# One first transfer cut into four, and a small one moved to the other queue

## The chip, the cores and the metric

The kernel runs on 1 core of one Trainium2 chip. The metric is the device time of one execution, in microseconds (us). Before the change it is 245.59 us, the median of 3 runs (245.19 to 245.89).

## The reference, cut to what matters

One block of a decoder works on one new token for each of 4 sequences: D is 512, there are 32 query heads, 8 heads of keys and values, a window of the last 2048 cached positions, and a hidden width of 1792. Everything is float32.

```python
mod = (_silu(c) @ w_mod).reshape(c.shape[0], 6, 1, -1)
sa, ca, ga, sb, cb, gb = (mod[:, i] for i in range(6))
h = _layernorm(x) * (1 + ca) + sa
x = x + ga * attention(h, k_cache, v_cache, wq, wo)
h = _layernorm(x) * (1 + cb) + sb
x = x + gb * ((_silu(h @ w1) * (h @ w3)) @ w2)
```

With four tokens there is little arithmetic for each byte of the weights and of the cache. What the change touches is the way in which the first weights, w_mod's part for sa and ca, reach the core together with x and c.

## The kernel before, in words

All large operands pass through one ring of buffers, the pool `stream`, with SLOTS = 5 tiles of 128 partitions by 8192 floats (4 MB each), all with the tag "w". `plan` (line 47) lists them in the order of their use: wma (sa and ca of w_mod, 128 x 4096), the two halves of wq, then for each of the 8 groups of heads its keys and its values, with the two halves of wo in between, then wmb, w1, w3, wmc and w2. `load_ahead(name)` (line 56) issues transfers on SP's queue until five tiles from the named one on have been asked for; a tile whose slot is still in use waits, on SP, until the last reader of that slot is done. So the first call, for wma, issues wma, wq0, wq1, k0 and v0, and each further call issues one more. `cuts` splits a tile's transfer by columns into several: w3 comes in two halves and w2 in four pieces (`W3_CUTS`, `W2_CUTS`, lines 23 and 24). All other tiles come in one transfer with whole rows; a row of wma has 4096 floats, 16 KB, and one of wq, k or v 32 KB. The host has laid all arrays out so that a tile is one block of 128 rows.

x and c lie side by side in one array of 128 x 144 floats, `xc_in`. It is loaded into `xc_sb` by ACT's queue (line 77), beside SP's first transfer.

The work at the front goes in this order. DVE and GpSimd make the constants (`ident`, `same`, `avg`, `pick`, zeros). When xc_sb has landed, ACT takes exp(-c) (line 111) and DVE makes from it sc, which is silu(c) (lines 112 to 114), and the row sums of x (line 163). `norm` gives mean and variance of x with two products (lines 120 and 126). `mod_columns` (line 154) multiplies sc with wma in 16 products, over 4 blocks k of the 512 inputs and 4 blocks j of columns: the columns of wma are ordered by k first, so that a quarter of its columns is one k. `modulate` and `transposed` make hT (line 151), and only then does `project_q` (line 172) use wq. Then come the 8 groups: scores (line 204), softmax, values (line 232). After them come the output projection (line 193), the second norm, the two products of the hidden layer (line 283), wmc's product, and the last product with w2 (line 311), whose result is added and stored.

Every execution of line 64 is one transfer on SP's queue, and they are served in the order of their issue.

Of the kernel before, what the change touches and what calls it, by code (L numbers as in the profile page):

```python
# [8 lines left out]
F32 = mybir.dt.float32  # L9
# [5 lines left out]
P = 128  # L15
# [3 lines left out]
ROW = 8192  # L19
# [9 lines left out]
def block_kernel(ctx: ExitStack, tc: tile.TileContext, xc_in, w_mod_a, w_mod_b, w_mod_c, wq, k_t, v, wo, w1, w3, w2, out):  # L29
# [4 lines left out]
    nc = tc.nc  # L34
# [3 lines left out]
    stream = ctx.enter_context(tc.tile_pool(name="stream", bufs=SLOTS))  # L38
# [14 lines left out]
    plan += [("wmb", w_mod_b, None), ("w1", w1, None), ("w3", w3, W3_CUTS), ("wmc", w_mod_c, None), ("w2", w2, W2_CUTS)]  # L53
    tiles = {}

    def load_ahead(name):

        upto = [n for n, _, _ in plan].index(name) + SLOTS
        for n, src, cuts in plan[len(tiles) : upto]:
            t = stream.tile([P, ROW], F32, tag="w", name="w")  # L60
            size = src.shape[1]
            for a, b in zip(cuts[:-1], cuts[1:]) if cuts else ((0, 1),):
                step = size // cuts[-1] if cuts else size
                nc.sync.dma_start(t[:, a * step : b * step], src[:, a * step : b * step])
            tiles[n] = t[:, :size]
        return tiles[name]
# [7 lines left out]

    nc.scalar.preload_act_table_set("natural_log_exp_and_others")
    xc_sb = consts.tile([P, P + 16], F32, name="xc_sb")
    nc.scalar.dma_start(xc_sb, xc_in)
    x_sb, ct_sb = xc_sb[:, :P], xc_sb[:, P:]

    wma = load_ahead("wma")  # L80


# [103 lines left out]
    for half in range(2):  # L186
        wq_t = load_ahead(f"wq{half}")
        for i in range(4):
            project_q(4 * half + i, wq_t[:, i * 2048 : (i + 1) * 2048])
# [5 lines left out]
    def group(g):  # L195
        nonlocal wo_t
        q = qT[:, g]
        kv = load_ahead(f"k{g}").rearrange("p (t b n) -> p t b n", t=NT, b=B)
        mx = small.tile([P, NT], F32, name="mx")
        s_t = []  # L200
# [160 lines left out]
```

## Time and profile before

| what | us |
|---|---|
| median of 3 runs | 245.59 (245.19 to 245.89) |
| the profiled execution | 245.65 |
| its span, first to last instruction | 243.9 |
| TensorE (PE) busy | 170.2 |
| VectorE (DVE) busy | 51.3 |
| ScalarE (ACT) busy | 34.6 |
| first issue of w_mod_a on SP, first issue of xc on ACT | 0.73, 0.76 |
| first work on xc_sb | 9.16 |
| first product with wq | 18.79 |
| issue of the store of the result | 241.49 |

The span is what the views of the trace show; the time of the execution has 1.75 us more, outside of the instructions. In the views, a row of groups of work names the line, the engine and the operands ("L204 PE MATMUL s<-w,qT"). A "DMA" step in the chain of waits goes from the issue of a transfer to the moment at which it lets its reader go, and so holds the time that it stood in the queue. In the windows view a row gives, for a stretch of time, how long each engine was busy, with the number of its instructions, then the granted clock of TensorE, the busy share of the 16 DMA engines and the rate. A packet is counted, with its bytes and its whole duration, in the stretch in which it starts, so that a short stretch can show a share above 1.

### The profile page before, as it was taken

The numbers are of one execution on the slowest core, as the hardware profiler recorded it, in microseconds if no ns is written. First come the engines' busy times: TensorE is split into PE (matmuls) and PEld (weight loads), VectorE is DVE, ScalarE is ACT, GpSimd is POOL, SyncE is SP. The second block draws the span as 40 slices with busy tenths as digits, with TensorE's granted clock in tenths as the row PEclk, the third lists the DMA queues.
The fourth block names the chain that finished last, engine by engine and source line by source line (L and its number), as shares of the span: only waits on it lengthen the run. The fifth ranks groups of instructions, "written<-read, shape, count | busy, mean of one in ns | idle before, by whom it ended". The sixth has DMA issues, their size and how long they took to land.

```text
span 243.9 us, 2815 instructions
## 1 busy us (share of the span) xinstructions
PE 170.2 (70%) x1194; PEld 71.2 (29%) x1194; DVE 51.3 (21%) x163; ACT 34.6 (14%) x90; POOL 2.2 (1%) x9
## 2 busy tenths in 40 slices
PE   0178788789696969783867549677655654865984
PEld 0123353351334323341253002421321210232242
DVE  1330000003334151511231003312311400123210
ACT  2000100100404022040040000400400400000000
POOL 3000000000000000000000000000000000000000
PEclk9995555555998999998579575797995996795899
DMA  7999999999999999999999999999999999999991
GB/s 238 462 430 430 430 430 427 430 430 430 430 423 430 430 427 430 430 431 427 441 430 427 435 435 441 430 427 435 430 430 435 441 422 411 435 416 433 415 413 69
DMA packets 4619, 101.49 MB, mean 416 GB/s; under 512 B 512, under 2 KB 768, under 8 KB 1024
## 3 DMA queue, kind: packets, MB, share of 16 engines
q1 hardware_dynamic: 4464, 101.26, 97.1%
q8 instruction: 9, 0.15, 0.2%
q10 hardware_dynamic: 144, 0.07, 0.1%
q14 instruction: 2, 0.02, 0.0%
HBM read 101.26 MB, written 0.07 MB: 416 GB/s over the span
## 4 chain that ended last, share of the span: by engine, by line
DMA 53%; PE 39%; ACT 4%; DVE 2%; issue 1%; SPq 0%; ACTq 0%
DMA w<-k_t 18%; DMA w<-v 17%; DMA w<-w 10%; PE s L204 10%; PE o_ps L232 9%; DMA w<-wq 7%; PE bank L175 6%; PE bank L180 6%; PE bank L228 5%; ACT q_sb L177 2%; PE bank L244 2%; ACT p_sb L218 1%; DVE mx L205 1%; ACT o_sb L240 1%; PE y_ps L311 1%
## 5 line engine op out<-in xcount | busy, mean ns | idle before, releaser
L204 PE MATMUL s<-w,qT 128*32 128x512 f32 x256 | 40.1, 783 | 14.4 <-DMA w<-k_t 14.4
L232 PE MATMUL o_ps<-w,pT 128*16 128x512 f32 x256 | 32.2, 648 | 6.7 <-DMA w<-v 6.7
L228 PE MATMUL bank<-ident,p_sb 128*128 128x128 f32 x128 | 23.7, 329 | 15.4 <-ACT p_sb L218 15.2
L218 ACT ACTIVATE p_sb<-s,nm 128x512 f32<-128x512 f32 x32 | 21.6, 687 | 82.3 <-DVE nm L208 82.3
L205 DVE TENSOR_REDUCE mx<-s 128x1 f32<-128x512 f32 x32 | 22.1, 692 | 45.8 <-PE s L204 45.8
L228 PEld LDWEIGHTS bank<-ident,p_sb 128*128 128x128 f32 x128 | 17.2, 165 | 26.9 <-ACT p_sb L218 26.8
L204 PEld LDWEIGHTS s<-w,qT 128*32 128x32 f32 x256 | 9.2, 139 | 39.2 <-issue 23.5
L180 PEld LDWEIGHTS bank<-same,q_sb 128*128 128x128 f32 x64 | 14.3, 328 | 19.9 <-ACT q_sb L177 19.9
L180 PE MATMUL bank<-same,q_sb 128*128 128x4 f32 x64 | 15.0, 357 | 6.1 <-ACT q_sb L177 6.1
L175 PE MATMUL bank<-w,hT 128*32 128x512 f32 x64 | 15.5, 1058 | 0.7 <-DMA w<-wq 0.7
L232 PEld LDWEIGHTS o_ps<-w,pT 128*16 128x16 f32 x256 | 6.9, 102 | 27.4 <-issue 19.3
L241 DVE TENSOR_SCALAR o_sb<-o_ps,rl 128x256 f32<-128x256 f32 x8 | 3.9, 483 | 44.1 <-ACT o_sb L240 44.1
L244 PE MATMUL bank<-pick,o_sb 128*128 128x16 f32 x64 | 9.1, 268 | 5.1 <-ACT o_sb L240 5.1
L193 PE MATMUL a_ps<-w,oT 128*4 128x512 f32 x64 | 9.8, 758 | 3.6 <-DMA w<-wo 3.3
L229 DVE COPY pT<-bank 128x64 f32<-128x64 f32 x32 | 7.2, 224 | 24.3 <-PE bank L228 24.3
L244 PEld LDWEIGHTS bank<-pick,o_sb 128*128 128x128 f32 x64 | 8.3, 190 | 12.5 <-ACT o_sb L240 12.5
L240 ACT ACTIVATE o_sb<-o_ps,rl 128x256 f32<-128x256 f32 x8 | 3.8, 474 | 50.3 <-PE o_ps L232 50.3
L283 PE MATMUL pg<-w,h2T 128*4 128x512 f32 (+3 forms) x64 | 9.8, 654 | 0.4 <-DVE h2T L151 0.4
L177 ACT ACTIVATE q_sb<-bank 128x512 f32<-128x512 f32 x8 | 4.8, 597 | 34.3 <-PE bank L175 34.3
L120 PE MATMUL bank<-tot,avg 128*128 128x1 f32 x4 | 0.9, 304 | 12.2 <-DVE avg L89 10.6
L181 DVE COPY qT<-bank 128x64 f32<-128x64 f32 x8 | 1.8, 225 | 34.9 <-PE bank L180 34.9
L159 PE MATMUL bank<-w,sc 128*4 128x256 f32 (+5 forms) x96 | 8.4, 441 | 0.5 <-DVE sc L114 0.5
(75 smaller groups left out, 54.0 us busy)
## 6 DMA issues: line engine op xcount, KB each, us to landing
w<-k_t SPq DMA_DIRECT2D x8, 4096.0 KB, 39.7
w<-v SPq DMA_DIRECT2D x8, 4096.0 KB, 40.1
w<-wq SPq DMA_DIRECT2D x2, 4096.0 KB, 22.1
w<-wo SPq DMA_DIRECT2D x2, 4096.0 KB, 40.9
w<-w SPq DMA_DIRECT2D x1, 3584.0 KB, 41.2
w<-w SPq DMA_DIRECT2D x2, 1792.0 KB, 35.7
w<-w_mod_b SPq DMA_DIRECT2D x1, 3072.0 KB, 40.9
w<-w_mod_a SPq DMA_DIRECT2D x1, 2048.0 KB, 8.2
```

Of the source, the lines that this page charges most:

```text
L159: nc.tensor.matmul(pb[32 * j : 32 * j + rows(k), : n * P], sc[:, k, : rows(k)], wv[:, k, j, :], start=(k == 0), stop=(k == 3))
L175: nc.tensor.matmul(qp[32 * k : 32 * k + 32, :], hT[:, k, :], wt[:, k * 512 : (k + 1) * 512], start=True, stop=True)
L177: nc.scalar.mul(q_sb, qp, DH**-0.5)
L180: nc.tensor.matmul(qtp[:, i, :], q_sb[:, i * P : (i + 1) * P], same[:, :B], start=True, stop=True)
L193: nc.tensor.matmul(a_ps[32 * i : 32 * i + B, :], oT[:, g, i, :], wo_t[:, g % 4, i, :], start=(g == 0), stop=(g == G - 1))
L204: nc.tensor.matmul(s[32 * b : 32 * b + 32, :], q[:, b, :], kv[:, t, b, :], start=True, stop=True)
L205: nc.vector.reduce_max(mx[:, t : t + 1], s, axis=AX.X)
L218: nc.scalar.activation(p_sb[:, t, :], s_t[t], AF.Exp, bias=nm, accum_out=ls[:, t : t + 1])
L228: nc.tensor.transpose(pt[:, c * P : (c + 1) * P], p_sb[:, t, c * P : (c + 1) * P], ident)
L232: nc.tensor.matmul(o_ps[32 * b : 32 * b + NC * R, :], pT[:, t, b].rearrange("p c r -> p (c r)"), vt[:, t, b, :], start=(t == 0), stop=(t = ...
L244: nc.tensor.matmul(otp, o_sb[:, c * P : (c + 1) * P], pick[:, c].rearrange("p r b -> p (r b)"), start=(c == 0), stop=(c == NC - 1))
L283: nc.tensor.matmul(pg[32 * j : 32 * j + rows(k), :n], h2T[:, k, : rows(k)], ws[:, k, j * 512 : j * 512 + n], start=(k == 0), stop=(k == 3))
```

## The change

A new function `load_first` takes the first tile out of the ring, fills it by four transfers on SP's queue, each with a quarter of the columns of w_mod_a (128 rows of 1024 floats, 4 KB), and then issues the transfer of x and c on the same queue. ACT issues none. The tile is entered under the name wma, so that `load_ahead("wma")` that follows issues wq0, wq1, k0 and v0, as it did after wma before. Nothing else is changed.

```diff
+    def load_first():
+        t = stream.tile([P, ROW], F32, tag="w", name="w")
+        size = w_mod_a.shape[1]
+        for i in range(4):
+            nc.sync.dma_start(t[:, i * size // 4 : (i + 1) * size // 4], w_mod_a[:, i * size // 4 : (i + 1) * size // 4])
+        nc.sync.dma_start(xc_sb, xc_in)
+        tiles["wma"] = t[:, :size]
+
     def load_ahead(name):
...
     xc_sb = consts.tile([P, P + 16], F32, name="xc_sb")
-    nc.scalar.dma_start(xc_sb, xc_in)
     x_sb, ct_sb = xc_sb[:, :P], xc_sb[:, P:]
 
+    load_first()
     wma = load_ahead("wma")
```

## The prediction, made before the result was known

> **What bounds the kernel now.** I read the page first: the span, the busy times, the line of the DMA engines, and what the queues carried.
>
> ```profile
> span 243.9 us, 2815 instructions
> PE 170.2 (70%) x1194; PEld 71.2 (29%) x1194; DVE 51.3 (21%) x163; ACT 34.6 (14%) x90; POOL 2.2 (1%) x9
> DMA  7999999999999999999999999999999999999991
> GB/s 238 462 430 430 430 430 427 430 430 430 430 423 430 430 427 430 430 431 427 441 430 427 435 435 441 430 427 435 430 430 435 441 422 411 435 416 433 415 413 69
> q1 hardware_dynamic: 4464, 101.26, 97.1%
> ```
>
> No engine is busy all the time, but the DMA engines are: nine tenths or more in every slice except the first and the last. SP's queue (q1) carries 101.26 MB, at about 430 GB/s in the middle. Only the first slice (238 GB/s over 6.1 us) and the last are low. So the time is the start of the transfers, plus the bytes over the rate, plus what follows the last landing. Next, the chain of waits, to see where TensorE hangs on these transfers.
>
> ```profile
> 1.16 17.49 DMA w<-wq
> ...
> 102.38 44.10 DMA w<-k_t
> ...
> 214.54 24.50 DMA w<-w
> ...
> 239.08 1.27 PE y_ps L311 x40
> ...
> 240.37 0.45 PE y_ps L311 x8
> ```
>
> TensorE waits for wq until 18.65, runs on its own chain until 102.38, and from there on it waits for transfers. A chain step of 44.10 us "DMA" is not one slow transfer: it is a transfer queued behind four others (4096 KB at 430 GB/s is 9.8 us each). The end hangs on the last pieces of w2, at 239.08 and again at 240.37.
>
> Does the queue ever run dry, so that an issue time matters? SP's timeline has the issues:
>
> ```profile
> 0.73 0.38 SPq L64 DMA_DIRECT2D w<-w_mod_a  x1
> 1.16 0.90 SPq L64 DMA_DIRECT2D w<-wq  x2
> 2.10 0.80 SPq L64 DMA_DIRECT2D w<-k_t  x1
> 2.94 0.65 SPq L64 DMA_DIRECT2D w<-v  x1
> 16.27 0.33 SPq L64 DMA_DIRECT2D w<-k_t  x1
> 34.15 0.33 SPq L64 DMA_DIRECT2D w<-v  x1
> 52.20 0.33 SPq L64 DMA_DIRECT2D w<-k_t  x1
> ```
>
> Before the issue at 52.20, 2048 KB and six times 4096 KB are queued, 27.3 MB; at 430 GB/s no more than 22.4 MB can have moved by then. About 4.8 MB are left, 11 us of work, and I find no shorter stock before the last loads. TensorE's first 100 us may thus shift by several us either way, and the landings stay where they are. What moves the end is what moves the queue itself: its first microseconds and its packets.
>
> **The change part by part.** The start, in the windows view (last two columns: DMA share, which counts a packet whole where it starts, and GB/s):
>
> ```profile
> 1.70:2.30 0.60, 0.00 (x0) 0.00 (x0) 0.29 (x1) 0.31 (x1) 0.60 (x1) 1.00 2.19 437
> 2.30:3.10 0.80, 0.00 (x0) 0.00 (x0) 0.00 (x0) 0.00 (x0) 0.40 (x2) 1.00 0.00 0
> 3.10:3.40 0.30, 0.00 (x0) 0.00 (x0) 0.00 (x0) 0.00 (x0) 0.00 (x0) 1.00 0.59 66
> 3.40:3.80 0.40, 0.00 (x0) 0.00 (x0) 0.00 (x0) 0.00 (x0) 0.00 (x0) 1.00 1.46 588
> 4.40:7.80 3.40, 0.00 (x0) 0.00 (x0) 0.00 (x0) 0.00 (x0) 0.00 (x0) 1.00 0.95 404
> 17.60:27.20 9.60, 7.33 (x32) 3.69 (x32) 0.59 (x3) 1.19 (x2) 0.00 (x0) 0.57 1.00 433
> ```
>
> In 1.70:2.30, 437 GB/s times 0.6 us is 262 KB: one 16 KB row of w_mod_a on each of the 16 engines. They take 2.19 x 0.6 = 1.31 us in the mean. At 404/0.95 = 425 GB/s a row of 16 KB takes 0.62 us, so the first one loses 0.70. No packet starts in 2.30:3.10. In 3.10:3.40 the few rows that start are nearly all those of x and c (66 GB/s is 20 KB, one long row and some short ones), and the second long rows come in 3.40:3.80 (235 KB, 14 of them). Taking the middles of the windows, 2.0 to 3.6, with 0.65 us for one long and one short row, the start loses 0.95 us, about 1.0: **0.70 in the first reads and some 0.3 around the first rows of x and c.**
>
> *The rows of 4 KB.* No transfer of before has them; the nearest packets are those of 2 KB at the end and of 32 KB in the middle. The DMA view from 238.60 to 239.30:
>
> ```profile
> DMA packets 75, 0.13 MB, mean 187 GB/s; under 512 B 11, under 2 KB 11, under 8 KB 75
> ...
> q1 hardware_dynamic: 75, 0.13, 49.7%
> ```
>
> 64 packets of 2 KB and 11 semaphore writes share 0.497 x 0.7 x 16 = 5.57 us, at most 87 ns each. A 32 KB row at 433 GB/s is 1211 ns. The straight line through both has 12 ns for a packet and 37.5 ns per KB: 4 KB is 162 ns, 16 KB is 612 (the window of w_mod_a gave 620). Four for one cost 4 x 162 - 612 = 36 ns more, and an engine has eight rows: **+0.29 us**, with the three further completions in it. Bounds: 0 (a 4 KB packet pays nothing) and 0.58 (twice the line, if the strided rows are read worse).
>
> *The first reads.* I keep the 0.70: it is a wait of an engine's first read, and the first row of 4 KB will meet it too. Bounds: all of it goes, because three further small rows are in flight behind the first (-0.70), or the same again is lost (+0.70).
>
> *x and c off ACT's queue.* Their 128 rows take the engines' time on either queue, so the bytes cost the same. What goes is the wedge ahead of the second long row: **-0.3 us**, bounds -0.3 and 0. The sum for the queue is 0.29 - 0.3 = -0.01 us, nothing.
>
> *When x and c arrive.* These rows give the landings and the front chain:
>
> ```profile
> w<-w_mod_a SPq DMA_DIRECT2D x1, 2048.0 KB, 8.2
> xc_sb<-xc_in ACTq DMA_DIRECT2D x1, 72.0 KB, 8.4
> ...
> 9.16 0.22 ACT L111 ACTIVATE e<-xc_sb 128x16 f32<-128x16 f32 x1 [7.15 <-DMA xc_sb<-xc_in]
> ...
> 11.68 1.06 PE L159 MATMUL bank<-w,sc 128*32 128x256 f32 x2 [0.47 <-DVE sc L114]
> ...
> 18.10 0.29 DVE L151 COPY hT<-bank 128x128 f32<-128x128 f32 x1 [0.42 <-PE bank L149]
> 18.79 1.90 PE L175 MATMUL bank<-w,hT 128*32 128x512 f32 x8 [0.73 <-DMA w<-wq]
> ```
>
> Today x and c take turns with w_mod_a and land with it: 0.73 + 8.2 = 8.9 and 0.76 + 8.4 = 9.2. In one queue they come behind its last row: the same end of the same bytes, 9.2 within 0.5. So the early landings of the first quarters buy nothing, since the first product of L159 needs sc, which is made from c. hT, now at 18.39, stays within that half microsecond, and wq is there at 18.65: the start of L175 moves by 0 to 0.3 us. All of it lies under the stock of 11 us or more.
>
> *The issues on SP.* Three more for w_mod_a and one for xc stand ahead of wq, k and v: at 0.38 to 0.80 us each, wq's issue goes from 1.16 to between 2.6 and 4.3. Until about 8 the engines have w_mod_a. That is hidden by some 4 us. If that cover were gone (an issue of over 1.5 us), the queue would gap by the excess. ACT loses one issue; its next work waits for xc anyway. The slots do not change: five tiles ahead, as before.
>
> One rule of the Trainium skill speaks against the cut. "DMA: Bandwidth & Descriptors" puts a fixed cost of about 2 us on each transfer (section "Anatomy of one DMA", there for GpSimd's path) and asks for at least 1 MiB each (section "Rules for kernel authors"). If that cost were paid in turn, its estimate for four pieces instead of one is 6 us more. The trace does not bear it out for queued pieces: w2's quarter-megabyte pieces, below, land with no such steps.
>
> ```profile
> 214.16 1.75 SPq L64 DMA_DIRECT2D w<-w  x4
> ...
> w<-w SPq DMA_DIRECT2D x1, 1024.0 KB, 24.5
> w<-w SPq DMA_DIRECT2D x2, 256.0 KB, 24.8
> ```
>
> The four pieces of w2 are issued some 0.44 us apart (1.75 / 4). The second, issued at about 214.6, lands at 239.1; the third and fourth, issued at about 215.0 and 215.5, land at 240.1 in the mean. That is 1.0 us later, where their bytes alone take 0.6 and 1.2 us, 0.9 in the mean: no two microseconds each.
>
> **The sum.** The profiled execution took 245.65 us, 1.75 more than its span of 243.9, and the median of the runs is 245.59, so it is a typical one. 245.65 - 0.01 gives 245.6.
>
> **The rivals.**
>
> *The whole start-up loss goes.* If several small reads in flight hide the first one, the 1.0 us goes and 0.29 comes: -0.7. The landings are set by the slowest engine, and late engines may gain more than the mean, another 0.3 by the spread of the second starts (3.1 to 3.8): 245.65 - 1.0 = 244.6. For it: 0.80 us in which not one packet starts is long, and the rows before and after it show that engines with one read outstanding stand still together. Against: an engine that waits for its first bytes waits at any row size.
>
> *Each quarter pays a start.* If every transfer opened with the 0.70 of the first, three more would give +2.1: 247.7. Against: the slices of 430 GB/s hold many boundaries between transfers without a dip.
>
> *A window of half clock falls on the tail.* This is the case that I hold against my forecast on the slow side. Four rows of the windows at the end, where the column ahead of the DMA share is the granted clock, and one of TensorE's waits:
>
> ```profile
> 220.00:222.00 2.00, 0.59 (x2) 0.50 (x2) 1.07 (x6) 0.46 (x2) 0.00 (x0) 0.56 1.05 444
> ...
> 224.00:226.00 2.00, 2.00 (x15) 0.43 (x10) 0.00 (x0) 0.00 (x0) 0.00 (x0) 0.50 1.00 423
> 226.00:228.00 2.00, 2.00 (x18) 0.48 (x14) 0.00 (x0) 0.00 (x0) 0.00 (x0) 0.73 0.96 392
> 228.00:230.00 2.00, 2.00 (x14) 0.52 (x6) 0.42 (x1) 0.37 (x1) 0.00 (x0) 1.00 1.05 441
> PE y_ps L311 <- DMA w<-w: 0.4, 1, 0.4
> ```
>
> Half clock (0.50 in the row between) lasts from about 220.2 to 227.1, some 6.9 us. The last product of w2 then waits only 0.4 us for its transfer. If the start shifts the work against these stretches so that one lasts half as long again, 3.4 us, TensorE loses 1.7, of which 0.4 is slack: +1.3, 246.9. It decides as soon as the loss passes 0.4 us. For it: the tail is that tight. Against: the three runs shown lie within 0.7 us. The Trainium skill ("TensorE: Matmul & The Clock Gate", Part 1) has windows of 3.4 us that run freely and do not start with the kernel; by that, such a loss would come and go between runs of before too, and their small spread agrees that it seldom does.
>
> **How the numbers follow.** About 0.3% (0.74 us) is what a measurement of this kernel can tell from no change. My forecast, 245.6, has 0.60; its bounds, with the spread of the runs, are 245.2 to 246.3. The start-up loss gone, 244.6, has 0.25 and is faster by over 0.3%. The half clock has 0.10 and the four starts 0.05, both slower. So faster 0.25, same 0.60, slower 0.15. The range takes in the forecast and the first rival with the runs' spread of 0.3, and leaves out 0.15: 244.3 to 246.4.
>
> **What would show it.** Right: a dead stretch after the first packets about as long as now; w_mod_a's last quarter and xc landing within 0.5 us of 9; 430 GB/s from there; w2's landings within 0.5 us of 239.04 (214.54 + 24.50) and 240.37. The first rival: packets starting between 2.3 and 3.1, and wq landing by 17.9 or so. The four starts: gaps at each quarter and wq at 20 or later. The half clock: w2 landed before TensorE gets to it. I would be wrong if the queue ran dry behind the longer row of issues, or if 4 KB rows at a stride of 16 KB moved much slower than the line says.

## The result, and the profile after

The changed kernel takes 246.69 us, the median of 6 runs (246.21 to 246.91), against 245.3 us for the kernel before, the median of 6 runs that include the three above. The ratio over all these runs is 1.004, with a 95% interval of 1.0024 to 1.0056: 0.6 to 1.4 us slower. The two medians lie 1.4 apart, at the upper end of that interval; later runs of the unaltered changed kernel give 1.0038. I had forecast no change, 245.6, and a range up to 246.4. By the ratio the time is 246.3 (1.004 of 245.3), at the edge of that range; the median lies 0.3 above it. Most of the interval lies beyond the 0.3% that I had taken for what a measurement of this kernel can tell from no change.

The profiled execution took 246.62 us. Its page, first the lines that answer to those of before:

```profile
span 244.8 us, 2820 instructions
PE 166.4 (68%) x1194; PEld 70.2 (29%) x1194; DVE 51.4 (21%) x163; ACT 34.6 (14%) x90; POOL 2.1 (1%) x9
...
DMA  6999999999999999999999999999999999999991
GB/s 222 460 428 428 434 434 431 428 428 428 434 432 428 428 426 428 444 426 424 434 434 420 439 434 434 434 426 439 428 439 431 423 428 418 430 419 427 418 388 48
...
q1 hardware_dynamic: 5040, 101.33, 97.0%
```

The picture is the same, with the DMA engines full from the second slice to the last but one. The first slice has gone from 238 to 222 GB/s: over 6.1 us that is 0.1 MB, or 0.2 us at full rate. Now the front of the timeline:

```profile
0.74 1.79 SPq L60 DMA_DIRECT2D w<-w_mod_a  x4
...
2.57 0.74 SPq L61 DMA_DIRECT2D xc_sb<-xc_in  x1
...
3.35 1.01 SPq L72 DMA_DIRECT2D w<-wq  x2
...
9.32 0.22 ACT L119 ACTIVATE e<-xc_sb 128x16 f32<-128x16 f32 x1 [7.31 <-DMA xc_sb<-xc_in]
...
17.04 0.29 DVE L159 COPY hT<-bank 128x128 f32<-128x128 f32 x1 [0.42 <-PE bank L157]
...
19.13 1.94 PE L183 MATMUL bank<-w,hT 128*32 128x512 f32 x8 [2.13 <-DMA w<-wq]
```

x and c land at 9.3 instead of 9.2, and hT is ready earlier, at 17.3 instead of 18.4, since the vector engine had made its constants before x came (from 1.9 us on; in the kernel before from 9.8). That gains nothing, for wq is later: the first product with it starts at 19.13 instead of 18.79, after a wait of 2.13 us. Then the chain of waits at its end:

```profile
161.05 43.97 DMA w<-v
205.01 0.04 issue
...
213.71 23.10 DMA w<-w
236.81 0.14 issue
236.94 4.57 PE y_ps L319 x112
241.51 0.02 issue
241.53 0.30 DVE y L321
```

The last values land at 205.02 (161.05 + 43.97) instead of 204.77 (in the kernel before, the product that waits for them starts at 204.81), and the multiplication by gb starts at 241.53 instead of 240.84. So the queue is 0.25 to 0.35 us late from the front to the tail, and the tail adds 0.4. The tail's own reason stands in the windows view, whose third column from the end is the granted clock:

```profile
234.00:237.00 3.00, 1.29 (x38) 0.91 (x41) 0.51 (x2) 0.00 (x0) 0.00 (x0) 0.86 0.97 405
237.00:240.00 3.00, 3.00 (x68) 2.66 (x72) 0.00 (x0) 0.00 (x0) 0.00 (x0) 0.57 0.66 255
```

In the kernel before the same stretch has the full clock:

```profile
237.00:240.00 3.00, 2.57 (x98) 2.26 (x91) 0.00 (x0) 0.00 (x0) 0.00 (x0) 1.00 0.57 216
```

A stretch of half clock fell on the last group of products (0.57 from 237 to 240). This was my third rival, and it is in this profile. Whether it is the cause is a question for the experiments.

The start of the queue, in the windows in which the prediction read it:

```profile
1.70:2.30 0.60, 0.00 (x0) 0.00 (x0) 0.60 (x5) 0.31 (x1) 0.60 (x1) 1.00 0.73 164
2.30:3.10 0.80, 0.00 (x0) 0.00 (x0) 0.65 (x8) 0.00 (x0) 0.40 (x2) 1.00 1.02 210
3.10:3.40 0.30, 0.00 (x0) 0.00 (x0) 0.00 (x0) 0.00 (x0) 0.00 (x0) 1.00 0.50 150
3.40:3.80 0.40, 0.00 (x0) 0.00 (x0) 0.00 (x0) 0.00 (x0) 0.00 (x0) 1.00 0.97 338
4.40:7.80 3.40, 0.00 (x0) 0.00 (x0) 0.00 (x0) 0.00 (x0) 0.00 (x0) 1.00 1.01 389
...
5.00:7.00 2.00, 0.00 (x0) 0.00 (x0) 0.00 (x0) 0.00 (x0) 0.00 (x0) 1.00 1.01 373
```

The dead stretch from 2.3 to 3.1 us is gone: packets start in it. But they run at half the rate, and by 3.8 us no more has been started than before (0.45 MB against 0.52, each row's rate times its length). New is the last row. Between 5 and 7 us the engines are occupied (1.01), yet they move 373 GB/s; in the kernel before the same row reads:

```profile
5.00:7.00 2.00, 0.00 (x0) 0.00 (x0) 0.00 (x0) 0.00 (x0) 0.00 (x0) 1.00 1.02 432
```

### The profile page after: what moved, and what is told of

The parts are those of the page before. It is cut to its first block, busy times and chain, and to the rows that moved or that the text cites. A ratio compares the mean times of both kernels' runs of the same rounds, so it can differ in the third digit from the quotient of the medians.

```text
span 244.8 us, 2820 instructions
## 1 busy us (share of the span) xinstructions
PE 166.4 (68%) x1194; PEld 70.2 (29%) x1194; DVE 51.4 (21%) x163; ACT 34.6 (14%) x90; POOL 2.1 (1%) x9
## 4 chain that ended last, share of the span: by engine, by line
DMA 64%; PE 29%; ACT 3%; DVE 1%; SPq 1%; issue 1%; ACTq 0%
DMA w<-k_t 30%; DMA w<-v 18%; DMA w<-w 9%; DMA w<-wq 6%; PE bank L183 6%; PE bank L188 6%; PE s L212 6%; PE o_ps L240 5%; PE bank L236 2%; ACT q_sb L185 2%; PE y_ps L319 2%; SPq L60 1%; ACT p_sb L226 1%; DVE mx L213 1%; PE bank L252 0%
## 5 line engine op out<-in xcount | busy, mean ns | idle before, releaser
L212 PE MATMUL s<-w,qT 128*32 128x512 f32 x256 | 38.1, 750 | 14.1 <-DMA w<-k_t 14.1
L240 PE MATMUL o_ps<-w,pT 128*16 128x512 f32 x256 | 31.4, 634 | 8.6 <-DMA w<-v 8.5
L236 PE MATMUL bank<-ident,p_sb 128*128 128x128 f32 x128 | 22.7, 313 | 15.4 <-ACT p_sb L226 15.2
L236 PEld LDWEIGHTS bank<-ident,p_sb 128*128 128x128 f32 x128 | 15.7, 156 | 27.5 <-ACT p_sb L226 27.5
L240 PEld LDWEIGHTS o_ps<-w,pT 128*16 128x16 f32 x256 | 6.8, 101 | 28.4 <-issue 18.4
L201 PE MATMUL a_ps<-w,oT 128*4 128x512 f32 x64 | 9.3, 721 | 4.9 <-DMA w<-wo 4.6
```

The source lines that it names most:

```text
L201: nc.tensor.matmul(a_ps[32 * i : 32 * i + B, :], oT[:, g, i, :], wo_t[:, g % 4, i, :], start=(g == 0), stop=(g == G - 1))
L212: nc.tensor.matmul(s[32 * b : 32 * b + 32, :], q[:, b, :], kv[:, t, b, :], start=True, stop=True)
L236: nc.tensor.transpose(pt[:, c * P : (c + 1) * P], p_sb[:, t, c * P : (c + 1) * P], ident)
L240: nc.tensor.matmul(o_ps[32 * b : 32 * b + NC * R, :], pT[:, t, b].rearrange("p c r -> p (c r)"), vt[:, t, b, :], start=(t == 0), stop=(t = ...
```

## The experiments

Four theories were tried. **Packets:** the 512 small packets of 4 KB cost the queue about 0.3 us, wherever they stand. **Queue:** moving x and c behind w_mod_a on SP's queue costs. **Transfers:** each further transfer costs while the queue starts. **Tail:** the half clock on the last group is what makes the kernel slow. Two measures are read beside the time. One is the rate from 5 to 7 us. The other is the start of the first product with the last values (o_ps of the last group of heads), which comes 0.04 us after their landing: some 200 us into a queue that never runs dry, it says how late the whole queue is. The expectations also name the start of the first product with wq; in again_before and late_four that product waits for hT and not for wq, so there it says less. All results in one table, below the kernel before in the order of the ratio; the rates are the last column of the row 5.00:7.00 of each kernel's windows, and the last three columns are read from one profile of each kernel.

| kernel | first loads | ratio to before (95%) | GB/s, 5 to 7 us | first product with wq, us | last values, us |
|---|---|---|---|---|---|
| before, first profile | 1 transfer, 16 KB rows, xc on ACT | 1 | 432 | 18.79 | 204.81 |
| halves_sp | 2 transfers, 8 KB rows, xc on SP | 0.9993 (0.9983 to 1.0003) | 422 | 18.35 | 204.23 |
| again_before | as before, unaltered | 0.9997 (0.9984 to 1.001) | 416 | 18.68 | 204.35 |
| one_sp | 1 transfer, 16 KB rows, xc on SP | 1.0002 (0.9982 to 1.0021) | 442 | 18.53 | 204.34 |
| late_four | as before, half of wq in 4 | 1.0011 (0.9996 to 1.0026) | 424 | 18.95 | 204.88 |
| pad_act | 1 transfer, 4 KB packets | 1.0013 (0.9997 to 1.0029) | 420 | 18.85 | 204.62 |
| pad8_act | 1 transfer, 2 KB packets | 1.0018 (1.0007 to 1.0029) | 410 | 19.05 | 204.72 |
| packed_sp | 4 transfers, 4 KB rows, blocks | 1.003 (1.0007 to 1.0054) | 326 | 19.31 | 205.32 |
| four_act | 4 transfers, 4 KB rows, xc on ACT | 1.0031 (1.0014 to 1.0048) | 379 | 19.34 | 205.36 |
| warm_after | changed kernel, tail kept busy | 1.0032 (1.002 to 1.0044) | 356 | 19.32 | 205.33 |
| again_after | changed kernel, unaltered | 1.0038 (1.0024 to 1.0052) | 313 | 19.55 | 205.59 |
| the changed kernel | 4 transfers, 4 KB rows, xc on SP | 1.004 (1.0024 to 1.0056) | 373 | 19.13 | 205.06 |
| eight_sp | 8 transfers, 2 KB rows, xc on SP | 1.0073 (1.0045 to 1.0101) | 319 | 20.57 | 206.08 |
| part4_sp | 4 transfers by partitions | 1.0181 (1.016 to 1.0202) | 246 | 22.57 | 208.53 |

### One half of the change alone: four_act and one_sp

four_act keeps the four transfers and gives x and c back to ACT:

```diff
-        nc.sync.dma_start(xc_sb, xc_in)
...
+    nc.scalar.dma_start(xc_sb, xc_in)
```

> The four transfers of 4 KB rows alone; x and c stay on ACT's queue. If the small packets cost the time (the packet theory), the first product with wq starts at about 19.1 as in the changed kernel (18.79 before) and the time is 0.3 to 1.0 us over before, as the changed kernel's. If the queue of x and c costs it (the queue theory), the first product with wq starts at 18.8 and the time is within 0.2 us of before.

one_sp does the other half:

```diff
-        for i in range(4):
-            nc.sync.dma_start(t[:, i * size // 4 : (i + 1) * size // 4], w_mod_a[:, i * size // 4 : (i + 1) * size // 4])
+        nc.sync.dma_start(t[:, :size], w_mod_a)
```

> w_mod_a in one transfer of 16 KB rows, with x and c behind it on SP's queue. Packet theory: no small rows, so first product with wq at 18.5 to 18.8 and the time within 0.3 us of before. Queue theory: the whole rise of the changed kernel, 0.7 to 1.4 us over before. My prediction's term of -0.3 us for the removed wedge would show here alone: wq at 18.5, 0.3 us under before.

four_act took 1.0031 of before (1.0014 to 1.0048), one_sp 1.0002 (0.9982 to 1.0021). The cut carries the rise. The queue of x and c alone costs no more than 0.5 us by the interval, where the queue theory wanted 0.7 to 1.4; that theory falls. The two lines of the last values, four_act first, then one_sp, with the DMA for which TensorE waited in brackets:

```profile
205.36 5.23 PE L240 MATMUL o_ps<-w,pT 128*16 128x512 f32 x26 [6.95 <-DMA w<-v]
```

```profile
204.34 4.97 PE L239 MATMUL o_ps<-w,pT 128*16 128x512 f32 x32 [4.98 <-DMA w<-v]
```

A whole microsecond lies between the two queues, and x and c behind w_mod_a stand with the earlier one. In one_sp's chain wq lets its reader go at 18.40, 0.25 before the 18.65 of the kernel before:

```profile
1.63 16.77 DMA w<-wq
```

That is the size of my term of -0.3, but the time shows nothing of it, and again_before, which changes nothing, is as early at the last values.

### Small packets without further transfers: pad_act and pad8_act

A destination whose blocks lie 16 floats apart cuts each row of one single transfer into packets of 4 KB (pad8_act: 2 KB), with x and c on ACT as before.

```diff
+        v = t[:, : cuts * (n + 16)].rearrange("p (k s) -> p k s", k=cuts)[:, :, :n]
+        nc.sync.dma_start(v, w_mod_a.rearrange("p (k s) -> p k s", k=cuts))
```

> One transfer, cut into packets of 4 KB by a destination whose four blocks lie 16 floats apart; x and c on ACT's queue. Packet theory: the same 512 packets of 4 KB as in the changed kernel, so first product with wq at 19.0 to 19.1, 0.3 us over before at the least. If the number of transfers is what costs (each opens with a start of its own), within 0.2 us of before.

> One transfer in packets of 2 KB (eight blocks 16 floats apart), x and c on ACT: the packets of eight_sp without its eight transfers. Packet theory: by the line, 0.34 to 0.4 us over pad_act, about 0.6 us over before, wq at 19.2 to 19.4. Transfer theory: eight_sp's rise of 1.8 us comes from its transfers, and this one is within 0.4 us of before.

pad_act took 1.0013 (0.9997 to 1.0029), some 0.3 us, though its interval reaches to no change; pad8_act took 1.0018 (1.0007 to 1.0029), some 0.4 us. Their rates from 5 to 7 us are undisturbed; pad_act's row:

```profile
5.00:7.00 2.00, 0.00 (x0) 0.00 (x0) 0.51 (x4) 0.00 (x0) 0.00 (x0) 1.00 1.02 420
```

So the packets cost about what the straight line gave for 4 KB. For 2 KB it gave 0.67, and the interval of pad8_act, 0.2 to 0.7, just reaches to it. The first product with wq came 0.15 us (pad_act) before the earliest time that the packet theory had named for it, and as much in pad8_act. The packets make a third of the changed kernel's rise, perhaps. The rest is not in the size of the packets.

### More transfers, and transfers of another shape: eight_sp and part4_sp

eight_sp has `range(8)` and eighths of the columns in the loop of `load_first`.

> Eight transfers with rows of 2 KB, x and c behind them on SP. Packet theory: by the line of 12 ns for a packet, 8 rows x 7 further packets x 12 ns = 0.67 us on the queue against before, so first product with wq at 19.4 to 19.5 and 0.4 us over the changed kernel. Transfer theory: seven further starts, wq at 20 or later. If neither counts, the same as the changed kernel.

part4_sp cuts by partitions instead:

```diff
-            nc.sync.dma_start(t[:, i * size // 4 : (i + 1) * size // 4], w_mod_a[:, i * size // 4 : (i + 1) * size // 4])
+            nc.sync.dma_start(t[32 * i : 32 * i + 32, :size], w_mod_a[32 * i : 32 * i + 32, :])
```

> Four transfers again, but cut by partitions (32 rows of 16 KB each), x and c behind them on SP's queue: the number of transfers of the changed kernel without its small packets. Packet theory alone: as one_sp, the first product with wq at 18.5 to 18.8 and the time within 0.2 us of before. Transfer theory (each further transfer costs the queue some 0.1 us while it starts): wq at 18.9 to 19.1 and 0.3 to 0.6 us over before.

eight_sp took 1.0073 (1.0045 to 1.0101), 1.8 us. Against pad8_act, with the same packets in one transfer, that is 1.35 us more (1.0073 - 1.0018 of 245.5), and its last values are 1.36 us later:

```profile
206.08 4.47 PE L240 MATMUL o_ps<-w,pT 128*16 128x512 f32 x20 [5.14 <-DMA w<-v]
```

This speaks for the transfer theory, and so does the first product with wq, which it had at 20 or later. part4_sp, meant to show four transfers without small packets, does not answer that: it met another limit, at 4.4 us (0.0181 of 245.5). While its quarters move, the rate is about half:

```profile
5.00:7.00 2.00, 0.00 (x0) 0.00 (x0) 0.00 (x0) 0.00 (x0) 0.00 (x0) 1.00 1.16 246
7.00:9.00 2.00, 0.00 (x0) 0.00 (x0) 0.00 (x0) 0.00 (x0) 0.00 (x0) 1.00 0.91 188
```

246 and 188 are 217 GB/s in the mean. The Trainium skill has it ("SBUF — State Buffer", section "Door 1: The DMA port swizzle"): the rate goes by how many of the 16 ports the partitions of a transfer reach, and its formula gives 8 ports for 32 adjoining partitions. Half of its ceiling of 435 GB/s is 217.5, an estimate by that page, and the trace agrees.

### Is it the pitch of the rows? packed_sp

A quarter by columns reads rows of 4 KB that lie 16 KB apart. packed_sp lays w_mod_a out on the host so that each quarter is one block of 512 KB; transfers and packets stay the same.

```diff
-            nc.sync.dma_start(t[:, i * size // 4 : (i + 1) * size // 4], w_mod_a[:, i * size // 4 : (i + 1) * size // 4])
+            nc.sync.dma_start(t[:, i * size // 4 : (i + 1) * size // 4], w_mod_a[i])
...
-        "w_mod_a": a(wm[:, :, :2].transpose(1, 0, 3, 2, 4)).reshape(P, 4096),
+        "w_mod_a": a(wm[:, :, :2].transpose(0, 1, 3, 2, 4)).reshape(4, P, 1024),
```

> The changed kernel, with w_mod_a laid out on the host so that each quarter is one block of 512 KB: the same four transfers and the same packets of 4 KB, but no rows 16 KB apart. Pitch theory (a quarter by columns reads badly because its 4 KB rows lie 16 KB apart): the slow stretch between 5 and 7 us goes, the first product with wq starts at 18.8 to 18.9, and the time is as pad_act's, 1.0005 to 1.002 of before. Transfer theory (each further transfer costs while the queue starts, however its rows lie): the slow stretch stays, wq at 19.1 to 19.6, 1.003 to 1.004.

It took 1.003 (1.0007 to 1.0054), and the slow stretch is there in full:

```profile
5.00:7.00 2.00, 0.00 (x0) 0.00 (x0) 0.00 (x0) 0.00 (x0) 0.00 (x0) 1.00 0.93 326
```

The pitch is not the cause of that stretch, and the rise stays, 0.7 us, though its interval of 0.2 to 1.3 leaves room for a part of it. The pitch does count at the very start: from 2 to 4 us packed_sp moves 371 GB/s, where the changed kernel has 236, packed_sp first:

```profile
2.00:4.00 2.00, 0.00 (x0) 0.00 (x0) 0.96 (x9) 0.01 (x1) 0.70 (x2) 1.00 0.96 371
```

```profile
2.00:4.00 2.00, 0.00 (x0) 0.00 (x0) 0.95 (x9) 0.01 (x1) 0.70 (x2) 1.00 0.90 236
```

What the quarters gain there as blocks of their own they lose again behind 4 us, since the last values come at 205.32, among the other kernels with four quarters. It is one profile, and why it is so is not shown.

### Fewer and later: halves_sp and late_four

halves_sp cuts w_mod_a in two instead of four. late_four leaves the start as it was and cuts the second half of wq, which moves between 18 and 28 us:

```diff
-    plan = [("wma", w_mod_a, None), ("wq0", wq[0], None), ("wq1", wq[1], None)]
+    plan = [("wma", w_mod_a, None), ("wq0", wq[0], None), ("wq1", wq[1], [0, 1, 2, 3, 4])]
```

> Two transfers with rows of 8 KB instead of four with 4 KB, x and c behind them on SP. Packet theory: 8 further packets of 12 ns on an engine, 0.1 us over one_sp. Transfer or pitch theory: about a third of the changed kernel's rise, 1.001 to 1.002 of before, wq at 18.7 to 19.0.

> The kernel before, with the second half of wq cut into four by columns (rows of 8 KB, 32 KB apart); it moves between 18 and 28 us, when the queue is full. Packet theory: 24 further packets on an engine, 0.3 us over before, 1.001. If a cut by columns costs at any time (pitch theory), the rate falls under 420 GB/s between 18 and 28 us and the time is 1.002 to 1.004. If it costs only where the queue starts (transfer theory), 1.000 to 1.001.

halves_sp was expected at 1.001 to 1.002 by the transfer theory and took 0.9993 (0.9983 to 1.0003): a second transfer of 1 MB costs nothing, so the price is not one for each transfer. Its row from 5 to 7 us:

```profile
5.00:7.00 2.00, 0.00 (x0) 0.00 (x0) 0.00 (x0) 0.00 (x0) 0.00 (x0) 1.00 1.01 422
```

late_four took 1.0011 (0.9996 to 1.0026), which the packets alone explain (0.3 us). Three further transfers of 1 MB in a full queue add nothing that shows, the rate from 18 to 28 us does not fall (451 GB/s, 423 in the kernel before), and SP had issued all four pieces of wq by 4.2 us, so the mere number of issues at the start is not it either. What costs is to cut the first 2 MB into pieces of 512 or 256 KB.

### The tail: warm_after and again_after

warm_after is the changed kernel with two products, whose result is not used, where TensorE waited for w2:

```diff
+    warm = bank()
+    for _ in range(2):
+        nc.tensor.matmul(warm, ident, qT.rearrange("p g b i -> p (g b i)")[:, :512], start=True, stop=True)
```

> The changed kernel with two products of 128x512 put ahead of the last group (their result is not used), where TensorE waited 1.7 us for w2 and then ran at half clock. Tail theory: the clock stays full there, the last group takes under 4 us from its first to its last product apart from its waits, and the time is 0.3 to 0.5 us under the changed kernel. If the tail's clock is chance and seldom met, the same as the changed kernel, or up to 0.7 us slower where TensorE had no time to spare.

> The changed kernel once more, unaltered, on the chip of these runs. If its rise is in the kernel: 1.002 to 1.006 of before again, with the first product with wq at 19.0 to 19.3. Its second profile shows whether the half clock on the last group comes back (tail theory: in some executions, and 0.4 us with it).

again_after took 1.0038 (1.0024 to 1.0052), warm_after 1.0032 (1.002 to 1.0044). warm_after is 0.15 us lower, with some 0.45 either way, so these runs alone do not exclude the 0.3 that the tail theory wanted. But warm_after's profile has the full clock from 237 to 240, and that execution took 246.50 us. And the end of again_after's chain shows that the rise comes without the half clock:

```profile
239.87 1.27 PE y_ps L319 x40
241.14 0.03 issue
241.17 0.45 PE y_ps L319 x8
241.61 0.02 issue
241.64 0.30 DVE y L321
```

The clock was full (40 products in 1.27 us, as before the change), and the kernel was as slow, 246.72 us in this execution: here the queue itself came 0.78 us late (205.59 against 204.81). The counterpart is halves_sp, whose profile has the half clock on the last group and which is not slower than before:

```profile
235.98 0.14 issue
236.12 4.54 PE y_ps L319 x112
```

The half clock comes and goes between profiles, and costs about 0.4 us where it comes (in the changed kernel's profile the last group began 0.54 us before again_after's at 237.48, and the end came 0.11 before). The tail theory falls as the cause of the whole rise. How often the half clock comes in each kernel is not known, so a small share of it is not excluded.

### What scatters by itself: again_before

> The kernel before, unaltered, under another name: how far a ratio and a profile scatter without any change. Expected 0.999 to 1.001, with the first product with wq at 18.5 to 18.9; if the starts of the queue scatter by themselves as much as they differ between the kernels (0.3 us and more), the differences in single profiles say nothing.

It took 0.9997 (0.9984 to 1.001), and its last values start at 204.35, where the first profile of the same kernel has 204.81. So single profiles of one kernel differ by up to 0.5 us in the landing, and only groups can be compared. The seven profiles with w_mod_a in one transfer or in two, both of the kernel before among them, stand between 204.23 and 204.88. The five with four quarters by columns stand between 205.06 and 205.59, 205.33 in the mean. eight_sp is at 206.08. The groups do not overlap. From the mean of before's two profiles, 204.58, the step to four is 0.75 us.

## Why the prediction was right in part, and the step that failed

**What bounds the kernel: right.** The end follows the queue. hT came 1.1 us earlier and changed nothing; a late queue came out at the end. I had hT within half a microsecond of its old time and had overlooked the constants. wq's issue on SP came at 3.35, between the 2.6 and 4.3 that I had given, and stayed hidden.

**The small packets, +0.29: about right.** pad_act measured +0.3 us, with an interval of -0.1 to +0.7.

**The wedge of x and c, -0.3: not confirmed.** one_sp, which has this step alone, measured 0.0 with half a microsecond on either side. The start still lost about as much as before.

**The first reads, 0.70 kept: right for a wrong reason.** I had read a wait in an engine's first read. With small rows packets do start in the dead stretch, which was my sign for the first rival, but they move at half the rate, and the queue gains nothing. The first half of my sign told of packets that start, and not of bytes that arrive; the second half, wq by 17.9, did not come (18.99, 3.35 + 15.64). Nor must a row of 4 KB meet such a loss: in packed_sp the first packets run at 371 GB/s from 2 to 4 us.

**The step that failed is the cost of the three further transfers, which the sum put at nothing beside their packets** ("+0.29 us, with the three further completions in it"). Its rival, "each quarter pays a start", had 0.05 and a price of +2.1 us. My reason against it was that "the slices of 430 GB/s hold many boundaries between transfers without a dip". Those boundaries lie in a full queue and between pieces of 1 MB and more, and late_four shows no cost of such a cut beside its packets. At the start, and with smaller pieces, there is one: with four pieces of 512 KB the rate falls to between 313 and 379 GB/s from 5 to 7 us in five profiles of five, against 410 to 442 in the seven that have one or two. Against the 432 of the kernel before, that is 53 to 119 GB/s less for two microseconds, 0.25 to 0.55 us of work at 430 GB/s; with the packets' 0.3 this estimate gives 0.55 to 0.85 us. The price is not one start each, as the rival had it, and its sign, wq at 20 or later, came among the cuts by columns with eight pieces only: two pieces cost nothing, four cost about 0.4 to 0.7 us beside their packets (0.003 to 0.004 of 245.5 is 0.7 to 1.0, less pad_act's 0.3), and eight 1.35. That the ratio's 246.3 still lies within my range is luck: the range reached up there by the bounds of other terms, packets at twice the line and a wedge that stays.

The rule of the Trainium skill that I set aside ("DMA: Bandwidth & Descriptors", section "Rules for kernel authors", at least 1 MiB for each transfer) is borne out at this place, by its size if not by its sum: halves of 1 MiB were free, quarters and eighths were not. The 6 us that its fixed cost would give, an estimate, are far from the 1.0 measured.

**The half clock on the tail, 0.10:** it did come, in the changed kernel's profile, and cost about 0.4 there. It also came in halves_sp, which is no slower than before, and it stayed away in the second profile of the changed kernel, which is. So it is not the reason for the difference. The two profiles of the kernel before do not have it on the last group.

**What stays open** is why pieces of 512 KB run slowly from about 5 us on. The number of transfers issued (late_four), the pitch of the rows (packed_sp), the size of the packets (pad_act) and the queue of x and c (four_act, one_sp) are excluded as the sole reason. The stretch stays when each quarter is one block on the host (packed_sp), and it is absent with the same packets in one transfer (pad_act). Whether it is the start that makes them slow, or their size anywhere, is not settled either: for the start speaks that w2's pieces of 256 KB landed by their bytes alone at the end of a full queue, in the kernel before; the quarters moved behind wq, into a full queue, were not tried.

## What to carry to other kernels

Where the DMA queue is full from the first microsecond to the last, the time is set by how soon it reaches full rate and by how many packets it carries; a reader that is ready earlier gains nothing when it then waits for the queue, as hT did here, 1.1 us early. Do not judge the start of a queue by its steady state: pieces of 512 and 256 KB cost 0.3 to 0.7% at the front, their packets included, where w2's small pieces at the end of a full queue showed no such price. And compare a queue's lateness far downstream, at a wait of which nothing but the queue decides, in several profiles, before half a microsecond is believed.

## What the runs showed of the hardware

Four transfers of 32 partitions each moved at 217 GB/s in the mean, against some 430 for transfers of 128 partitions, and cost the kernel 1.81% (1.6 to 2.02%). The other surprise: in the kernel before and in the changed one, the engines' first two microseconds (1.7 to 3.8) bring 0.52 and 0.45 MB, about half of the 0.90 that 430 GB/s would. With rows of 16 KB this looks like a stretch without packets, with rows of 4 KB like slow packets. It is no fixed loss: with each quarter in one block on the host, 4 KB packets moved 371 GB/s from 2 to 4 us (packed_sp), against 236 with rows 16 KB apart.
